# Inverse's input in two buffers, loaded 14 steps ahead; S before the filter in the ring; the last accumulator added by TensorE

## The chip, the cores and the metric

The kernel runs on one core of one Trainium2 chip. The metric is the device time of one execution in microseconds (us). Each execution computes the whole chain below once, from inputs in HBM to the output in HBM.

## The reference, cut to what matters

```python
X = np.fft.rfft(x, axis=1)                      # x: 8 x 3072 x 256, float32
y = np.fft.irfft(X * (filt_r + 1j * filt_i), n=3072, axis=1)
t = y.reshape(8 * 3072, 256)
h = np.maximum(t @ w_in, 0.0)                   # w_in 256 x 2048
z = h * h @ w_out                               # w_out 2048 x 256
logits = z @ phi                                # phi 256 x 32
d = softmax(logits, axis=0)                     # over all 24576 tokens
slot_in = (d.T @ z).reshape(8, 4, 256)          # 8 experts, 4 slots each
slot_out[e] = np.maximum(slot_in[e] @ w1[e], 0) @ w2[e]
out = softmax(logits, axis=1) @ slot_out
```

The softmax over tokens runs over the whole sequence of all batches, so the kernel carries a running maximum, a running sum and a running weighted accumulator, and rescales them as it goes.

## The kernel before, in words

The tokens go through in 48 chunks of 512, six to a batch of 3072 tokens. The main loop is over pairs: `pair(P)` does two of the sixteen 128-wide blocks of the hidden layer for a chunk, so a chunk has 8 pairs. Time inside the program is counted in steps, two to a pair, 16 to a chunk. TensorE always has the hidden layer to do (`layer`, lines 594 to 596, three passes each). Everything else is put between these matmuls by a written timetable: five lists of (step, function, arguments), called streams, are sorted by step, and `run_streams` emits what has come due. So the order of instructions on each engine is fixed when the program is built; at run time each engine works through its own list in that order, and waits where an instruction's input or buffer is not ready.

Around the hidden layer stand, by batch:

- the forward transform: `load_x` (line 143) brings x in, `mm_a` (165) transforms, `store_a` (181) writes the result S to HBM. S is read again in another layout by `load_s2` (206), the filter by `load_f2` (198), their small matrices by `load_w` (190). `mm_b` (299) does the second half, `filt` (310) multiplies by the filter, `join` (319) adds;
- the inverse: `load_v` (194) brings a matrix, `mm_g2` (218) does the first half, `store_g2` (240) writes the result G to HBM. Then, for each chunk, `load_g` (460) reads 512 KB of G into the tile `gin`; `mm_y` (514) does the last half, and `even_y`, `unfold`, `lead_y`, `rest_y` (522, 531, 539, 546) make of it the hidden layer's input `xo`. `mm_y` of a chunk stands 12 steps ahead of the chunk's first hidden block, `rest_y` ends 8.5 steps after `mm_y`;
- the dispatch (`dispatch_events`): the logits of a chunk (663), the softmax numbers, and `slot_in` (793), 32 matmuls that add the chunk's tokens into the 32 slots. They read the hidden values `hT` from a copy in another layout, `hd`, made by 16 DMAs of 256 KB a chunk (`move`, 651). `hd` has one buffer, so the first move of a chunk waits for `slot_in` of the chunk before. `accum` (853) adds the chunk into the accumulator `ac` on VectorE.

All these DMAs but a few are issued by SyncE (SP), one after the other in the order of the timetable. A DMA that has to wait for a buffer or for another DMA's landing holds all that stand behind it on SP.

Buffers that matter: `gin` has one in before (4 KB a partition). The tiles of x, filter, S and of the inverse's result share one tag, `f8`, with three buffers, so each takes the buffer of the third before it; the text calls this the ring. The table `LEAD` holds, for batch 1, batch 2 and all later ones, how many steps ahead of its use each of four loads is asked for: the small matrix, the inverse's matrix, the filter, S.

At the end (from line 1252) the last chunk's `slot_blocks` (810) leave four partial sums in PSUM. They are copied out (1295, 1297), `sum_block` (835) adds them into one PSUM bank `pst`, and VectorE forms `fin`, the accumulator times its scale plus `pst`. `turn_l` (759) turns the logits of the last chunk, `sT` is `fin` turned, and the matmuls of line 1318 read `sT`. The expert layers (1338, 1360) and the output (1405) follow. Weights of the experts are loaded into tiles that have come free.

Of the kernel before, what the change touches and what calls it, by code (L numbers as in the profile page):

```python
# [6 lines left out]
F32 = mybir.dt.float32  # L7
F32R = mybir.dt.float32r
U32 = mybir.dt.uint32
ACTF = mybir.ActivationFunctionType  # L10
ALU = mybir.AluOpType
# [4 lines left out]
D = 256  # L16
# [9 lines left out]
NS = 32  # L26
# [12 lines left out]
def body(tc, x, cA, cAf, fwp, fwd, ivp, inv, flt, cst, w_in, w_out, phi, w1, w2, out):  # L39
    nc = tc.nc  # L40
    sync = nc.sync
    act, vec, gps, pe = nc.scalar, nc.vector, nc.gpsimd, nc.tensor
# [7 lines left out]
    G = {}  # L50
# [6 lines left out]
    first_c, first = pool("first")  # L57
# [34 lines left out]
    ident = cst_t[:, C_ID:C_ID + 128]  # L92
# [361 lines left out]
    def out_events(b, st, late):  # L454

        def load_g(g):
            if b + g:
                t = G["mlp"].tile([128, 4, D], F32, tag="gin", name="gin")
                src, o = (st["G1"], 0) if (b, g) == (0, 1) else (st["G"], 4 * g - 8 * (b == 0))
                sync.dma_start(out=t, in_=src[:, o:o + 4, :])  # L460
            else:
                t = scratch("gi", 1, [128, 4, D])
                sync.dma_start(out=t[0:96], in_=st["Gu"])
                sync.dma_start(out=t[96:128], in_=st["Gz"])
            st["gi", g] = t
# [82 lines left out]
        for g in range(NCB):  # L548
            if 6 * b + g not in (0, 1, 6):
                T = 96 * b + 16 * g - 12  # L550
                late(T - 6.5, load_g, g)
                late(T, mm_y, g)
                late(T + 0.5, even_y, g)
                late(T + 1, unfold, g, ALU.add)
                late(T + 1.5, unfold, g, ALU.subtract)
                for k in range(2):
                    late(T + 5.5 + 2 * k, lead_y, g, k)
                    late(T + 6.5 + 2 * k, rest_y, g, k)
                continue
            T = 96 * b + 16 * g - 4  # L560
            put = late
            if T < 0:
                def put(t, fn, *a):
                    put0(ST["G0"] + ST["Gd"] * (t + 7), fn, *a)
            put(T - (5 if (b, g) == (0, 1) else 3), load_g, g)
            if T < 0:
                put(T - 1, warm)
            for k in range(2):
                put(T + k, mm_ai, g, k)
                put(T + k + 0.5, lead_ai, g, k)  # L570
                put(T + k + 0.5, rest_ai, g, k)
# [123 lines left out]
    run = {}  # L695

    def dispatch_events(c, put):
        q = 16 * (c + 1) + (2 if c else 6)
        st = {}
        dsp = G["dsp"]  # L700
# [127 lines left out]
                act.activation(out=t, in_=p, func=ACTF.Copy)  # L828
            done(p)

        def sum_block(r, p):
            t = st.pop(("sp", r))
            for n in range(4):
                rows = slice(32 * n, 32 * n + 32)
                pe.matmul(
                    p[rows, :].rearrange("p (f r j) -> p f r j", r=4, j=32)[:, :, r, :], s32,
                    t[:, 128 * n:128 * n + 128].rearrange("p (f j) -> p f j", j=32),
                    start=True, stop=True, skip_group_check=True, tile_position=(0, 32 * n),
                )

        def sum_blocks():
            st["S"] = p = side()
            for r in range(4):
                sum_block(r, p)

        def accum():
            p = st["S"]
            if "ac" not in run:
                run["ac"] = dsp.tile([128, 4 * 512], F32, tag="ac", name="ac")
            ac = run["ac"][:, 0:512]  # L850
            if "m" in run:
                z = dsp.tile([128, 1], F32, tag="z", name="z", bufs=2)
                vec.scalar_tensor_tensor(out=ac, in0=ac, scalar=st["sc"], in1=p, op0=ALU.mult, op1=ALU.add)  # L853
                vec.scalar_tensor_tensor(
                    out=z, in0=run["z"], scalar=st["sc"], in1=st["zb"], op0=ALU.mult, op1=ALU.add
                )
            else:
                vec.tensor_copy(ac, p)
                z = st["zb"]
            done(p)  # L860
            run["z"], run["m"] = z, st["nm"]
# [31 lines left out]
        if c == 0:  # L893
            put(q + 7.5, slot_blocks)
            for r in range(4):
                put(q + 9 + .5 * r, keep_block, r)
            put(q + 11.5, sum_blocks)
            put(q + 12, accum)
        else:
            put(q + 7.5, slot_in)  # L900
            put(q + 9, accum)
# [199 lines left out]
    with tc.manual_schedule():  # L1101
        put, late = stream("fft"), stream("late")
        st = {}
# [23 lines left out]
        for n in range(4):  # L1127
# [2 lines left out]
                wput(WO[n][1][k], conv_wo, n, k)  # L1130

        LEAD = [
            [[5.5] * 4, [3.5] * 4, [5.5] * 4, [5] * 4],
            [[5.5, 7.5, 15.25, 15.25], [6.5, 12.5, 13.5, 13.5], [5.5, 5.5, 10, 10], [5, 5, 9.5, 9.5]],
            [[20.25] + [15.25] * 3, [13.5] * 4, [20.5, 10, 10, 10], [8, 9.5, 9.5, 9.5]],
        ]

        opened = False
# [6 lines left out]
        for b in range(1, NB):  # L1145
            st = {}
# [8 lines left out]
        for c in range(NCH - 1):  # L1155
            dispatch_events(c, stream("dsp"))
            if c:
                for n in range(4):
                    t = 0.5 * (n // 2)
# [7 lines left out]
        dsp, mlp = G["dsp"], G["mlp"]  # L1167
# [4 lines left out]
        def bank(tag):  # L1172
            return G["ps"].tile([128, 512], F32, tag=tag, name="pt")
# [41 lines left out]
        for P in range(NP + 2):  # L1215
            if P == 11:
                open_fft()
            if P == 48 * (NB - 1):
                G["fft_c"].__exit__(None, None, None)
                G["w1_c"], w1p = pool("w1p")  # L1220
                for n in range(6):
                    m = 4 if n < 5 else 2
                    w1t.append(w1p.tile([128, m * 512], F32, tag=f"w{n}", name="w1t"))
                    load_experts(w1t[-1], m, 0)
            if P == NP - 7:
                early = G["mlp"].tile([128, 8 * D], F32, tag="xo", name="wx", bufs=2)
                load_experts(early, 0, 3)
                c_two = early[:, 3 * D:4 * D].rearrange("p (t s) -> p t s", s=NS)
                sync.dma_start(out=c_two, in_=c_dr[:, 0:8, :])
                sk = early[:, 4 * D:].bitcast(F32R).rearrange("p (g t a s) -> p g t a s", g=2, t=4, a=4)  # L1230
            if P > NP - 8:
                j, odd = divmod(P - NP + 7, 2)
                if odd:
                    for nm in "HL":
                        n1 = int(j == 0)
                        load_experts(wp.tile([128, 1024], F32, tag=f"i{nm}{j}", name="wx"), n1, 4 - 2 * n1)
            if P == NP - 4:
                big = G["dsp"].tile([128, FT * CH], F32, tag="hT", name="wx", bufs=1)
                load_experts(big[:, 0:4096], 8, 0)
                wor = big[:, 4096:].rearrange("p (f d) -> p f d", d=D)  # L1240
                for n in range(4):
                    sync.dma_start(
                        out=wor[32 * n:32 * n + 32],
                        in_=wo_dr[512 * n:512 * n + 512, :].rearrange("(k j) d -> j k d", j=32),
                    )
            if P == NP - 2:
                ct_two = mlp.tile([128, 2, 4, 128], F32R, tag="gin", name="ct")
                go(stack, stack)
            pair(P)

# [7 lines left out]
        for k in range(2):  # L1258
# [8 lines left out]
        slot_blocks()  # L1267
        go(keep, keep)
        hs = [[mlp.tile([128, 512], F32, tag=f"h{k}", name="hs", bufs=5) for k in range(2)]]
        vec.tensor_tensor(out=st["zb"], in0=st["zs"][:, 0:1], in1=st["zs"][:, 1:2], op=ALU.add)  # L1270
        fz = dsp.tile([128, 1], F32, name="fz")
        vec.scalar_tensor_tensor(
            out=fz, in0=run["z"], scalar=st["sc"], in1=st["zb"], op0=ALU.mult, op1=ALU.add
# [14 lines left out]
        for n in range(3):  # L1288
            load_call(n)
        pst = bank("L")  # L1290
        parts = hs[0] + [dsp.tile([128, 512], F32, tag=t, name="sp") for t in ("lp", "et")]
        for r in range(4):
            p = st["S"][r]
            if r % 2:
                vec.tensor_copy(parts[r], p)
            else:
                act.activation(out=parts[r], in_=p, func=ACTF.Copy)
            done(p)
            st["sp", r] = parts[r]
            sum_block(r, pst)  # L1300
        fin = dsp.tile([128, 512], F32, tag="eT", name="fin", bufs=2)
        vec.scalar_tensor_tensor(
            out=fin, in0=run["ac"][:, 0:512], scalar=st["sc"], in1=pst, op0=ALU.mult, op1=ALU.add
        )
        turn_l()
        sT = dsp.tile([128, 16, NS], F32, tag="lp", name="sT")
        vec.transpose(sT.rearrange("p f s -> p (f s)"), fin)
        load_experts(dsp.tile([128, 512], F32, tag="et", name="wx"), 0, 2)
        load_experts(dsp.tile([128, 4 * 512], F32, tag="ac", name="wx"), 0, 7)
        row_max()  # L1310
        row_exp()
        row_out()
# [2 lines left out]
        p = bank("s0")  # L1315
# [253 lines left out]
```

## Time and profile before

| | before |
|---|---|
| median of 3 runs | 1973.51 us (1968.02 to 1975.3) |
| the profiled execution's own time | 1969.8 us |
| its span, first to last instruction | 1968.0 us |
| mean granted TensorE clock (share of full speed) | 0.974 |
| TensorE busy (matmul) | 1855.7 us, 94% |
| VectorE, ScalarE, GpSimd busy | 61%, 52%, 39% |
| DMA busy share in the body | about 0.75 |

PE is TensorE's matmuls, PEld its weight loads, DVE VectorE, ACT ScalarE, POOL GpSimd, SP SyncE, SPq its DMA issues. A wait in square brackets is the idle time of the engine just ahead of an instruction, with the one that ended it. The granted clock has two levels here: 1.00 is 2.4 GHz and 0.50 is 1.2 GHz.

### The profile page before, as it was taken

To read this page: it belongs to the slowest core of one execution; us is meant where nothing else is said; L and a number is where in the kernel's file an instruction comes from. 1 tells how busy PE (TensorE), PEld (TensorE's weight loads), DVE (VectorE), ACT (ScalarE), POOL (GpSimd) and SP (SyncE) were. 2 spreads that over 40 slices of the span, in tenths; PEclk is the share of its full clock that TensorE was granted. 3 is DMA by queue.
4 is the path that set the end of the run, shared out by engine and by line. 5 is a ranking of instruction groups with operands and counts; after the bars stand their busy time and mean duration, and the time that the engine had idled before them with its cause. 6 is when DMAs were issued, how large, how long until landed. Compare 5 with 4: busy or idle time off the path is not lost.

```text
span 1968.0 us, 42096 instructions
## 1 busy us (share of the span) xinstructions
PE 1855.7 (94%) x16324; PEld 1220.7 (62%) x16324; DVE 1207.0 (61%) x2267; ACT 1033.2 (52%) x1930; POOL 773.7 (39%) x812
## 2 busy tenths in 40 slices
PE   8999999989999999989999999998998999899987
PEld 6656566656666666666665666666565666466555
DVE  7856556556656566556665566555665566455558
ACT  6755445545545465545554465454554455455535
POOL 4044444334435344434434444344443343233224
PEclk9999999999999999999999999999999999999989
DMA  8678779867866796777876696677867756664989
GB/s 298 215 196 234 224 203 263 230 180 214 257 180 176 193 276 178 218 219 211 254 205 166 173 275 198 176 218 205 261 180 202 205 136 196 194 171 125 232 322 379
DMA packets 245799, 425.04 MB, mean 216 GB/s; under 512 B 25696, under 2 KB 103648, under 8 KB 245600
## 3 DMA queue, kind: packets, MB, share of 16 engines
q1 hardware_dynamic: 244728, 421.13, 74.1%
q8 instruction: 130, 2.13, 0.4%
q10 hardware_dynamic: 728, 1.15, 0.2%
q14 instruction: 69, 0.57, 0.1%
q0 software_dynamic: 144, 0.07, 0.0%
HBM read 151.71 MB, written 77.59 MB: 117 GB/s over the span
## 4 chain that ended last, share of the span: by engine, by line
PE 68%; DMA 13%; SPq 8%; DVE 5%; issue 3%; ACT 2%; POOL 1%; DVEq 0%; POOLq 0%; ACTq 0%
PE p L594 15%; PE p L596 13%; PE p L595 13%; PE sd L793 8%; DMA gin<-G 8%; PE L L663 7%; SPq L651 4%; PE sd L514 3%; PE sd L299 3%; SPq L206 2%; PE sd L165 2%; DVE hT L622 2%; DMA f<-x 1%; ACT h L601 1%; PE sd L218 1%
## 5 line engine op out<-in xcount | busy, mean ns | idle before, releaser
L601 ACT ACTIVATE h<-p 128x512 f32<-128x512 f32 x768 | 458.7, 597 | 572.0 <-PE p L596 555.2
L605 POOL TENSOR_TENSOR h<-h 128x512 f32<-128x512 f32 x375 | 393.0, 1048 | 914.5 <-ACT h L601 820.1
L622 DVE STREAM_TRANSPOSE hT<-h 128x512 f32<-128x512 f32 x736 | 489.9, 693 | 370.9 <-ACT h L603 313.4
L594 PE MATMUL p<-xo,wiH 128*128 128x512 f32 x1534 | 636.0, 415 | 0.0
L596 PE MATMUL p<-xo,wiL 128*128 128x512 f32 x1534 | 613.1, 400 | 0.0
L595 PE MATMUL p<-xo,wiH 128*128 128x512 f32 x1534 | 613.0, 400 | 0.0
L594 PEld LDWEIGHTS p<-xo,wiH 128*128 128x128 f32 x1534 | 294.1, 192 | 158.9 <-issue 82.1
L596 PEld LDWEIGHTS p<-xo,wiL 128*128 128x128 f32 x1534 | 293.5, 191 | 69.9
L595 PEld LDWEIGHTS p<-xo,wiH 128*128 128x128 f32 x1534 | 294.6, 192 | 60.1
L603 ACT ACTIVATE h<-h 128x512 f32<-128x512 f32 x393 | 248.4, 632 | 12.5
L319 POOL TENSOR_TENSOR u<-u 128x256 f32<-128x256 f32 x224 | 160.7, 740 | 126.0 <-DVE u L310 126.0
L663 PE MATMUL L<-h,wf 128*32 128x512 f32 x1536 | 186.4, 599 | 2.2 <-DVE wf L1017 1.8
L793 PE MATMUL sd<-hd,eT 128*32 128x512 f32 x1472 | 169.1, 597 | 8.6 <-DMA hd<-hT 8.6
L310 DVE TENSOR_TENSOR u<-sd,f 128x512 f32<-128x512 f32 x240 | 152.8, 675 | 10.9 <-PE sd L299 9.2
L793 PEld LDWEIGHTS sd<-hd,eT 128*32 128x32 f32 x1472 | 48.3, 111 | 120.9 <-issue 106.3
L546 POOL TENSOR_TENSOR xo<-gin,xo 128x512 fp32r<-128x512 f32 x90 | 119.0, 1322 | 0.0
L514 PE MATMUL sd<-cst_t,gin 64*64 64x64 f32 x2880 | 60.5, 242 | 56.5 <-DMA gin<-G 56.5
L531 DVE TENSOR_TENSOR gin<-gin,sd 128x512 f32<-128x512 f32 x90 | 60.0, 667 | 86.7 <-ACT gin L522 79.9
L228 ACT ACTIVATE f<-sd 128x512 f32<-128x512 f32 x112 | 61.1, 610 | 86.4 <-PE sd L218 86.4
L514 PEld LDWEIGHTS sd<-cst_t,gin 64*64 64x64 f32 x2880 | 54.3, 154 | 73.9 <-issue 73.6
L853 DVE SCALAR_TENSOR_TENSOR ac<-ac,sc,sd 128x512 f32<-128x512 f32 x46 | 34.4, 748 | 107.1 <-PE sd L793 107.1
L663 PEld LDWEIGHTS L<-h,wf 128*32 128x32 f32 x1536 | 40.4, 109 | 95.1 <-issue 89.7
(159 smaller groups left out, 1600.2 us busy)
## 6 DMA issues: line engine op xcount, KB each, us to landing
hd<-hT SPq DMA_DIRECT2D x736, 256.0 KB
f<-flt SPq DMA_DIRECT2D x28, 1024.0 KB
gin<-G SPq DMA_DIRECT2D x47, 512.0 KB
out<-w1t SPq DMA_DIRECT2D x47, 512.0 KB
f<-x SPq DMA_DIRECT2D x84, 256.0 KB
S<-f SPq DMA_DIRECT2D x42, 512.0 KB
f<-S SPq DMA_DIRECT2D x112, 192.0 KB
G<-f SPq DMA_DIRECT2D x112, 192.0 KB
```

What stands on the lines that cost most here:

```text
L310: vec.tensor_tensor(out=u, in0=p.rearrange("p (h d) -> p h d", d=D), in1=f[:, 2 * r + k:2 * r + k + 1, :].to_broadcast([128, 2, D]), op=AL ...
L319: gps.tensor_tensor(out=a[:, h, :], in0=a[:, h, :], in1=b[:, 1 - h, :], op=ALU.add if h else ALU.subtract)
L514: pe.matmul(y.rearrange("p (q a t) -> p a q t", q=2, a=4)[:, a], t[rows, a, o:o + 64], cI[rows, 0:64], start=True, stop=True, skip_group_c ...
L594: pe.matmul(p, wh, x[:, 0, kk, :], start=(kk == 0), stop=False)
L595: pe.matmul(p, wh, x[:, 1, kk, :], start=False, stop=False)
L596: pe.matmul(p, wl, x[:, 0, kk, :], start=False, stop=(kk == 1))
L601: act.activation(out=h, in_=p, func=ACTF.Relu, scale=2.0 ** -8)
L603: act.activation(out=h, in_=h, func=ACTF.Square)
L605: gps.tensor_tensor(out=h, in0=h, in1=h, op=ALU.mult)
L622: vec.transpose(hT[c, f // 8][:, f // 4 % 2, :, o:o + 128], h2[P, k].rearrange("p (b t) -> p b t", b=4))
L663: pe.matmul(lg[c][32 * n:32 * n + 32, :], wf[:, f, :], h2.pop((P + n // 2, n % 2)), start=(f < 4), stop=(f >= FT - 4), tile_position=(0, 3 ...
L793: pe.matmul(S[32 * n:32 * n + 32, :], e[:, 32 * t:32 * t + 32], v, start=(t == 0), stop=(t == 3), tile_position=(0, 32 * n),)
```

## The change: what it does

1. `gin` gets two buffers, and `load_g` is asked for 14 steps ahead of `mm_y` in place of 6.5 (never before step 13.5). The chunks 0, 1 and 6, which go another way, keep their times.
2. `LEAD`: S is asked for ahead of the filter. In batch 1 by half a step, in batch 2 from its second stage on, and from batch 3 on in every stage but the first S comes 15.25 steps ahead (9.5 before) and the filter stays at 10. In batch 1 the filter goes from 5.5 to 5 steps ahead, S from 5 to 5.5.
3. The accumulator's tile shrinks from 8 to 4 KB a partition, which pays for `gin`'s second buffer. Expert weights that were loaded into its tail at the end go into the free `gin` buffer two pairs before the loop ends.
4. At the end the accumulator is scaled in place on VectorE, and TensorE puts it into `pst` with a matmul by the identity before the sums are added on top. `fin` is gone, `sT` is turned straight from `pst`, and `turn_l` stands behind it.
5. `accum` of the first chunk is called at the end of `sum_blocks`, half a step earlier.

```diff
         def load_g(g):
             if b + g:
-                t = G["mlp"].tile([128, 4, D], F32, tag="gin", name="gin")
+                t = G["mlp"].tile([128, 4, D], F32, tag="gin", name="gin", bufs=2)
...
-                late(T - 6.5, load_g, g)
+                late(max(T - 14, 13.5), load_g, g)
                 late(T, mm_y, g)
...
-        def sum_block(r, p):
+        def sum_block(r, p, first=True):
...
-                    start=True, stop=True, skip_group_check=True, tile_position=(0, 32 * n),
+                    start=first, stop=True, skip_group_check=True, tile_position=(0, 32 * n),
...
             for r in range(4):
                 sum_block(r, p)
+            accum()
...
-                run["ac"] = dsp.tile([128, 4 * 512], F32, tag="ac", name="ac")
+                run["ac"] = dsp.tile([128, 2 * 512], F32, tag="ac", name="ac")
...
-            put(q + 12, accum)
...
-            [[20.25] + [15.25] * 3, [13.5] * 4, [20.5, 10, 10, 10], [8, 9.5, 9.5, 9.5]],
+            [[20.25] + [15.25] * 3, [13.5] * 4, [20.5, 10, 10, 10], [8, 15.25, 15.25, 15.25]],
...
-                ct_two = mlp.tile([128, 2, 4, 128], F32R, tag="gin", name="ct")
+                ct_two = mlp.tile([128, 2, 4, 128], F32R, tag="gin", name="ct", bufs=2)
+                load_experts(mlp.tile([128, 4 * D], F32, tag="gin", name="wx", bufs=2), 0, 4)
...
+        ac = run["ac"][:, 0:512]
+        vec.tensor_scalar(out=ac, in0=ac, scalar1=st["sc"], scalar2=None, op0=ALU.mult)
...
         pst = bank("L")
+        pe.matmul(pst, ident, ac, start=True, stop=False, skip_group_check=True)
...
-            sum_block(r, pst)
-        fin = dsp.tile([128, 512], F32, tag="eT", name="fin", bufs=2)
-        vec.scalar_tensor_tensor(
-            out=fin, in0=run["ac"][:, 0:512], scalar=st["sc"], in1=pst, op0=ALU.mult, op1=ALU.add
-        )
+            sum_block(r, pst, False)
+        sT = dsp.tile([128, 16, NS], F32, tag="lp", name="sT")
+        vec.transpose(sT.rearrange("p f s -> p (f s)"), pst)
         turn_l()
-        sT = dsp.tile([128, 16, NS], F32, tag="lp", name="sT")
-        vec.transpose(sT.rearrange("p f s -> p (f s)"), fin)
...
-        load_experts(dsp.tile([128, 4 * 512], F32, tag="ac", name="wx"), 0, 7)
+        load_experts(dsp.tile([128, 2 * 512], F32, tag="ac", name="wx"), 0, 3)
```

Three places show how the instructions stand. The first is SP's list over one chunk of batch 3 with a filter in it, which repeats in three chunks of each batch; `hd<-hT` are the moves for `slot_in`, `gin<-G` the inverse's load, `f<-S` and `f<-flt` the loads of S and filter. Before:

```order
L651 DMA hd<-hT 128x1x512 x8
L198 DMA f_6351<-flt 128x2x1024
L206 DMA f_6358<-S 48x4x256 x4
L460 DMA gin<-G 128x1024
L651 DMA hd<-hT 128x1x512 x8
L879 DMA c_dr<-co 128x128
L194 DMA iv<-inv 128x256 x2
L240 DMA G<-f_6490 48x4x256 x4
L190 DMA fw<-fwd 48x256 x4
```

The same stretch of SP's list now:

```order
L651 DMA hd<-hT 128x1x512 x8
L198 DMA f_6358<-flt 128x2x1024
L651 DMA hd<-hT 128x1x512 x8
L880 DMA c_dr<-co 128x128
L194 DMA iv<-inv 128x256 x2
L240 DMA G<-f_6490 48x4x256 x4
L460 DMA gin<-G 128x1024
L190 DMA fw<-fwd 48x256 x4
L206 DMA f_6667<-S 48x4x256 x4
```

The loads of `gin` and of S have left the place between the two groups of moves and stand after the second, behind the store of G and ahead of the next chunk's moves.

The second place is SP's list at the end of a batch's forward work, where the store `G<-f` is the batch's last and the load `gin<-G` behind it now is the same batch's first. Now:

```order
L240 DMA G<-f_5330 48x4x256 x4
L460 DMA gin<-G 128x1024
L181 DMA S<-f_5207 128x1024 x2
L143 DMA f_5505<-x 64x2x512 x4
L143 DMA f_5518<-x 64x2x512 x4
L651 DMA hd<-hT 128x1x512 x8
```

Before, that load stood behind the eight moves; it reads what the store ahead of it writes, so SP now waits there for the store's landing.

The third place is VectorE's list at the end, after the copies of the last partial sums. Before, and then now:

```order
L1295 COPY sp<-sd 128x512
L1302 SCALAR_TENSOR_TENSOR fin<-ac,sc,pt 128x512
L759 STREAM_TRANSPOSE lt<-sd 32x128 x4
L1307 STREAM_TRANSPOSE sT<-fin 128x512
L779 TENSOR_REDUCE rm<-lt 128x4
```

```order
L1299 COPY sp<-sd 128x512
L1306 STREAM_TRANSPOSE sT<-pt 128x512
L759 STREAM_TRANSPOSE lt<-sd 32x128 x4
L779 TENSOR_REDUCE rm<-lt 128x4
L780 TENSOR_TENSOR cl<-lt,rm 128x128
```

`fin` has gone, and `sT` stands ahead of the four turns of the logits instead of behind them.

## Rows read from the trace of the kernel before

**Rows 1.** The page's head: span, then busy time and share of each engine.

```profile
span 1968.0 us, 42096 instructions
PE 1855.7 (94%) x16324; PEld 1220.7 (62%) x16324; DVE 1207.0 (61%) x2267; ACT 1033.2 (52%) x1930; POOL 773.7 (39%) x812
```

**Rows 2.** Waits of PE, whole span: us in total, times, longest us.

```profile
PE sd L514 <- DMA gin<-G: 56.5, 17, 5.7
PE sd L793 <- DMA hd<-hT: 8.6, 1, 8.6
...
PE sd L299 <- DMA f<-S: 3.2, 3, 2.5
```

**Rows 3.** Windows over the twelve half-clock stretches: the second, and the sum of all.

```profile
core 0: us, PE busy (x) PEld busy (x) DVE busy (x) ACT busy (x) POOL busy (x), PEclk, DMA share, GB/s
...
430.49:437.32 6.83, 5.24 (x72) 4.48 (x73) 1.03 (x2) 1.83 (x3) 0.00 (x0) 0.50 0.83 234
...
sum 64.86, PE 57.02 PEld 48.11 DVE 15.97 ACT 18.92 POOL 0.00; mean PE 4.75 PEld 4.01 DVE 1.33 ACT 1.58 POOL 0.00
```

**Rows 4.** Chain of waits in order of time, four slot_in: start us, us, what.

```profile
403.68 3.43 PE sd L793 x32
...
447.37 3.43 PE sd L793 x32
...
483.24 3.43 PE sd L793 x32
...
518.78 3.43 PE sd L793 x32
```

**Rows 5.** Timeline of SP, two stretches: start us, us, engine, line, what.

```profile
213.01 0.42 SPq L198 DMA_DIRECT2D f<-flt  x1
213.47 2.16 SPq L206 DMA_DIRECT2D f<-S  x4
...
407.18 8.22 SPq L651 DMA_DIRECT2D hd<-hT  x8
415.44 0.81 SPq L198 DMA_DIRECT2D f<-flt  x1
416.30 4.49 SPq L206 DMA_DIRECT2D f<-S  x4
420.89 0.41 SPq L460 DMA_DIRECT2D gin<-G  x1
421.40 11.45 SPq L651 DMA_DIRECT2D hd<-hT  x8
...
435.98 2.55 SPq L240 DMA_DIRECT2D G<-f  x4
```

**Rows 6.** Waits of SP's DMA queue, whole span: us in total, times, longest us.

```profile
SPq L651 <- PE sd L793: 324.3, 44, 12.2
SPq L651 <- DMA f<-flt: 56.8, 24, 4.7
...
SPq L206 <- DMA S<-f: 20.2, 10, 4.0
```

**Rows 7.** Timeline of PE in batch 1, with the wait ahead of it.

```profile
219.45 0.59 PE L299 MATMUL sd<-f,fw 48*32 48x256 f32 x2 [2.46 <-DMA f<-S]
```

**Rows 8.** Timeline of all engines at the end of the loop.

```profile
1861.41 1.13 PE L719 MATMUL sd<-lp,cst_t 128*128 128x512 f32 x2 [0.69 <-ACT lp L708]
...
1870.93 0.75 DVE L1302 SCALAR_TENSOR_TENSOR fin<-ac,sc,pt 128x512 f32<-128x512 f32 x1 [0.55 <-PE pt L835]
1871.59 1.28 DVE L759 STREAM_TRANSPOSE lt<-sd 32x128 f32<-32x128 f32 x4
...
1873.72 3.10 PE L1318 MATMUL pt<-wx,sT 128*32 128x256 f32 x32 [2.86 <-DVE sT L1307]
```

**Rows 9.** Windows over two other half-clock stretches, columns as in rows 3.

```profile
222.20:229.10 6.90, 6.37 (x41) 4.27 (x42) 2.63 (x6) 1.23 (x2) 2.83 (x4) 0.51 1.05 379
...
1874.33:1884.57 10.24, 9.34 (x59) 3.40 (x52) 3.40 (x7) 0.72 (x2) 0.00 (x0) 0.50 0.99 319
```

More of the change, by code (lines that the diff above doesn't have):

```diff
@@ L1132, in body @@
         LEAD = [
-            [[5.5] * 4, [3.5] * 4, [5.5] * 4, [5] * 4],
-            [[5.5, 7.5, 15.25, 15.25], [6.5, 12.5, 13.5, 13.5], [5.5, 5.5, 10, 10], [5, 5, 9.5, 9.5]],
-            [[20.25] + [15.25] * 3, [13.5] * 4, [20.5, 10, 10, 10], [8, 9.5, 9.5, 9.5]],
+            [[5.5] * 4, [3.5] * 4, [5] * 4, [5.5] * 4],
+            [[5.5, 7.5, 15.25, 15.25], [6.5, 12.5, 13.5, 13.5], [5, 5.5, 10, 10], [5.5, 13, 15.25, 15.25]],
+            [[20.25] + [15.25] * 3, [13.5] * 4, [20.5, 10, 10, 10], [8, 15.25, 15.25, 15.25]],
         ]
```

## The prediction

> **What bounds the kernel now.** I read the page first: TensorE (PE) is busy 1855.7 of 1968.0 us, and no other engine passes 62% [rows 1]. So PE sets the time, and the question is what its idle 112 us wait for. The list of PE's waits answers that: 56.5 us, half of it, is line 514 waiting for the load of `gin`, 17 times, at most 5.7 us; the next largest is one wait of 8.6 us for `hd` [rows 2]. The reader should see that this is one cause in one place of the timetable.
>
> The granted clock comes next. Behind twelve of the 17 waits it stands at 0.50 (1.2 GHz) for a stretch; the windows over these twelve stretches add up to 64.9 us, in which PE is busy 57.0 [rows 3]. Work done at 0.50 takes twice as long as at 1.00 (2.4 GHz), so half of the busy time, 28.5 us, is lost there, behind the waits and on top of them.
>
> The chain of waits checks this. From one slot_in to the next a chunk takes 43.7 us (403.68 to 447.37), the one after it 35.9, and the third 35.5 (483.24 to 518.78) [rows 4]. The first holds a wait for `gin`, the third holds none and does as much PE work (the hidden layer and two of the transform's pieces). The excess of 8.2 us is the 5.7 us wait plus 5.24 / 2 = 2.6 us of slow clock behind it [rows 2, 3].
>
> Why `gin` is late is in SP's timeline of that chunk: the first eight moves for slot_in are issued from 407.18, behind them the filter (1 MB), S and, at 420.89, `gin`; then eight more moves [rows 5]. Its 512 KB queue behind all these bytes and are wanted about 5 us before they are there.
>
> **The change, part by part.**
>
> *gin in two buffers, 14 steps ahead.* The load now stands behind the store of G (435.98 to 438.53 in that chunk [rows 5]) for the chunk after. A chunk without waits takes 35.5 us for 16 steps, 2.2 us a step; 14 steps are 31 us, against the some 14 us that 6.5 steps give now. The second buffer is free by then: the tile two before is done 8.5 steps after its own use, 9.5 steps ahead of this load. All 17 waits should go: 56.5 us. With them goes what follows them, 28.5 us. What is late next? After `gin` PE has no wait that comes again in every chunk [rows 2], so nothing waits close behind it; I book no new wait in the body, and put what could be there into the rivals.
>
> The Trainium skill speaks on the second term ("TensorE: Matmul & The Clock Gate", section on HAM oscillation): PE waiting on DMA is throttled to half its clock, and the penalty is half of the throttled time. By that rule the twelve stretches would give back 64.9 / 2 = 32.4 us, an estimate with that page, and the sum would be 3.9 us lower. The rows show less, since 64.9 - 57.0 = 7.8 us of the stretches lie in the waits themselves, which are counted already.
>
> *SP's new waits.* Nothing is added in DMAs; the 47 loads are the same. But the moved ones stand ahead of the moves now: S with 4.49 us and `gin` with 0.41 us of SP's time [rows 5] pass in front of the next chunk's first move. That move waits for slot_in anyway, 324.3 us in 44 waits, 7.4 us a chunk [rows 6]: this slack covers the 4.9 us. If it were gone, the moves would come up to 4.9 us later; but the second eight come as much earlier, since S and `gin` no longer stand in front of them. In 7 chunks (the first load of a batch) SP also waits for the landing of the store of G just ahead. The nearest row is S read back behind its own store: 20.2 us in 10 waits, 2.0 us each, 4.0 at most [rows 6]. Bounds 0 and 7 x 4.0 = 28 us of PE time; I take 0, since behind that place SP waits for slot_in too, and x, the load it holds, is folded steps later.
>
> Here a rule of the skill speaks against the change ("DMA: Bandwidth & Descriptors", on where the fixed cost of about 2 us goes): completion, above all of a write to HBM, makes up most of a DMA's fixed time, so waiting for a store is dear. By that page's figures the four stores of 768 KB would hold SP 2.0 us plus 1.8 us of moving, an estimate of 3.8 us. The row's longest, 4.0 us, agrees, and the sum stays, since 7.4 us of slack is more than either.
>
> *S ahead of the filter.* In batch 1 one second half of the transform waits 2.46 us for S [rows 7], whose load is issued 0.46 us behind the filter's 1 MB (213.01 and 213.47) [rows 5]; a half-clock stretch with 6.37 us of busy PE follows [rows 9]. Asked for first, S lands earlier by what the filter moves. Gain between 0 (the filter then holds VectorE's multiplication) and 2.5 + 6.4 / 2 = 5.6 us; I take 4, nearer to the upper end, since PE does not read the filter. From batch 3 on S moves out of the crowded stretch between the moves; PE waits for S only 3.2 us in the whole span [rows 2], so it saves nothing itself. In the ring S now takes the buffer of the S before it, as the loads ahead of it on SP wait for the same matmuls: no new wait.
>
> *First accum half a step earlier.* VectorE's order is the same; 0.
>
> *The end.* PE waits 2.86 us between the last sums and line 1318 [rows 8]. On the chain there, `fin` (0.75) and the turns of the logits (1.28) go away from in front of `sT`: 2.0 us. The new matmul by the identity has a like in line 719, the same shape and type: 1.13 us in two passes [rows 8]. It stands where PE waits for the copies of the partial sums, so it adds between 0 and 1.1 us; I take 0.5, the middle. Net 1.5 us, bounds 0.9 and 2.0. VectorE's scaling of `ac` runs while PE does the partial sums: 0. Behind this wait follows 10.24 us at half clock with 9.34 us of busy PE [rows 9], worth 4.7 us if the shorter wait no longer brings it on and 0 if it does; I take half, 2.3. The end gives 3.8 us, bounds 0.9 and 6.7.
>
> **The sum.** 56.5 + 28.5 + 4 + 3.8 = 92.8 us. The profiled execution took 1969.8 us (span 1968.0), so it would take 1877.0. The median of the runs shown is 3.7 us above the profiled execution, and I add this: 1880 us, 4.7% faster. Its own range: the two small terms at their upper ends (5.6 and 6.7) give 1876, and a few us more where other waits shrink along with these, 1870; the two at their lower ends give 1887, and one or two waits for `gin` that stay, 1892.
>
> **The rivals.**
>
> *The moves become the limit.* With shorter chunks slot_in may wait for `hd`. In the chunk of rows 5 SP finishes the second eight moves at 432.85 and slot_in starts at 447.37 [rows 4], 14.5 us later. The chunk loses 8.2 us, the moves gain 4.9 us on SP, so 11.2 us stay for landing: enough. Against that, SP is held by DMAs in flight: moves wait for the filter's landing 56.8 us in 24 waits [rows 6], and the filter now stands directly ahead of them. If the 4.9 us is not won, 14.5 - 8.2 = 6.3 us stay for landing and queueing, which is thin. Say the 18 chunks with a filter of batches 2 to 7 each wait 2.5 us: 45 us back, 1880 + 45 = 1925 us. Chance 0.15.
>
> *The load still comes late.* If SP reached the new place late, because the store of G ahead of it waits or because the loads share one queue, the waits would stay in part. Against it: 31 us of lead, and SP has 7.4 us to spare in each chunk. If half the waits and half of the slow clock stayed, 1880 + 42 = 1922; if nearly all, about 1965 (1880 + 85). Chance 0.06, most of it at the lower figure.
>
> *Slower.* One mechanism: SP's list is in order, and `gin` behind the store of G and S behind the matmuls that free its ring buffer hold the first moves of the next chunk until slot_in starves. The price is the wait seen once, 8.6 us [rows 2]: in the 18 chunks with a filter 155 us, so 1880 + 155 = 2035 us. It decides from 92.8 / 18 = 5.2 us a chunk on, and first the 7.4 us of slack must be used up. The delays listed, 4.9 us and in 7 chunks 2 to 4 us more, come close to the slack in those 7 only. Chance 0.04.
>
> *More than the sum.* The one wait of 8.6 us for `hd` [rows 2] goes too because the DMA traffic is spread, and the small terms are at their upper ends: 1876 - 8.6 and some slow clock behind it, about 1865. Chance 0.05.
>
> **How the numbers follow.** Forecast 0.70, moves 0.15, late load 0.06, slower 0.04, more 0.05. Predicted is the forecast's 1880. The range 1862 to 1918 holds the forecast, the better case and a part of the moves' case (those with up to 2.1 us a chunk); outside are the rest of that case, the late load and the slower one, some 0.18. A difference under 0.5% (10 us) cannot be told from none, the runs before spread 7 us. Faster: 0.70 + 0.15 + 0.05 and most of the late load, 0.94; same 0.02; slower 0.04.
>
> **What would show it.** In the profile after: no row, or a row of a few us, for line 514 waiting for `gin`; granted clock near 0.99 on average, and no half-clock stretch in the body but around batch 1 and the one `hd` wait; all chunks with a filter at 35 to 36 us from slot_in to slot_in; SP's wait of the moves for slot_in still there, about 2 us shorter; S in batch 1 no longer waited for; `sT` directly behind the sums, with line 1318 about 1.5 us nearer to them. The forecast is wrong if line 793 shows waits for `hd` in many chunks (moves), if line 514 keeps more than 15 us (late load), or if SP's first move of a chunk waits for nothing of slot_in any more.

## The result, and the profile after

The changed kernel took 1884.03 us (median of 4 runs, 1880.15 to 1886.42) against 1972.63 us of the kernel before (1968.02 to 1975.3): a ratio of 0.9551, 95% interval 0.9526 to 0.9576. The forecast was 1880, its range 1862 to 1918. The profiled executions differ by as much: spans of 1968.0 and 1878.2 us, 89.8 us apart.

The head of the page after (span, then busy time and share of each engine) answers to [rows 1]:

```profile
span 1878.2 us, 42103 instructions
PE 1824.0 (97%) x16326; PEld 1196.4 (64%) x16326; DVE 1206.0 (64%) x2267; ACT 1034.8 (55%) x1930; POOL 774.4 (41%) x812
```

PE did the same work (two matmuls more) in 31.7 us less of busy time, and idles 54.2 us where it idled 112.3. So 58.1 us of the gain is waiting that is gone, and 31.7 is work done at a higher clock. Apart from PE's own weight loads (PEld, 24.3 us less), no engine's busy time moved by more than 1.6 us.

What PE waits for after (us in total, times, longest us), against [rows 2]:

```profile
PE sd L793 <- DMA hd<-hT: 6.9, 1, 6.9
...
PE sd L723 <- DVE lo L712: 6.0, 7, 2.3
PE sd L218 <- DMA iv<-inv: 4.1, 2, 3.1
```

Line 514 and the load of `gin` are in the list no more: all 17 waits went. The longest one left is the single wait for `hd`. The half-clock stretches within the span add up to 23.6 us in five places, against 100.5 in eighteen. Line 723 waits 2.6 us more for VectorE than before (3.4).

The chain of waits in order of time (start, us, what) shows the chunk length, as in [rows 4]:

```profile
359.41 3.43 PE sd L793 x32
...
395.04 3.43 PE sd L793 x32
...
430.65 3.43 PE sd L793 x32
...
466.94 3.43 PE sd L793 x32
```

A chunk with a filter takes 35.6 us where 43.7 was seen before; it has become as long as the chunk without a wait (35.5). The one at 430.65, which loads x instead of a filter, takes 36.3.

SP's timeline of the first of these chunks, after, answers to [rows 5]:

```profile
362.91 8.32 SPq L651 DMA_DIRECT2D hd<-hT  x8
371.27 0.60 SPq L198 DMA_DIRECT2D f<-flt  x1
371.97 9.15 SPq L651 DMA_DIRECT2D hd<-hT  x8
...
384.01 2.46 SPq L240 DMA_DIRECT2D G<-f  x4
386.56 0.79 SPq L460 DMA_DIRECT2D gin<-G  x1
387.45 2.13 SPq L190 DMA_DIRECT2D fw<-fwd  x4
389.71 3.17 SPq L206 DMA_DIRECT2D f<-S  x4
398.53 2.58 SPq L651 DMA_DIRECT2D hd<-hT  x3
```

Between the two times eight moves only the filter is left; `gin` and S stand behind the store of G, and behind them SP has 5.7 us (392.9 to 398.5) in which it issues nothing. What SP's queue waits for, after, against [rows 6]:

```profile
SPq L651 <- PE sd L793: 252.2, 39, 11.1
...
SPq L206 <- DMA S<-f: 32.7, 12, 6.3
...
SPq L460 <- DMA G<-f: 15.6, 12, 2.8
SPq L651 <- DMA f<-flt: 15.0, 17, 2.0
```

The moves still wait for slot_in, 6.5 us each time (7.4 before). The wait for the store of G in front of `gin` is new. The moves' waits behind the filter fell from 56.8 to 15.0.

### The profile page after: what moved, and what is told of

Its sections match the earlier page's. It is cut to its first block, busy times and chain, and to the rows that moved or that the text cites. A ratio compares the mean times of both kernels' runs of the same rounds, so it can differ in the third digit from the quotient of the medians.

```text
span 1878.2 us, 42103 instructions
## 1 busy us (share of the span) xinstructions
PE 1824.0 (97%) x16326; PEld 1196.4 (64%) x16326; DVE 1206.0 (64%) x2267; ACT 1034.8 (55%) x1930; POOL 774.4 (41%) x812
## 4 chain that ended last, share of the span: by engine, by line
PE 84%; DMA 6%; DVE 3%; SPq 3%; issue 2%; ACT 1%; POOL 0%; DVEq 0%; ACTq 0%
PE p L594 18%; PE p L596 17%; PE p L595 17%; PE sd L793 9%; PE L L663 8%; PE sd L299 3%; PE sd L514 2%; PE sd L218 2%; PE sd L165 2%; SPq L651 2%; DMA f<-x 2%; DMA hd<-hT 1%; DMA f<-flt 1%; DVE ct L1204 1%; PE pt L1193 1%
## 5 line engine op out<-in xcount | busy, mean ns | idle before, releaser
L594 PE MATMUL p<-xo,wiH 128*128 128x512 f32 x1534 | 626.6, 408 | 0.0
L596 PE MATMUL p<-xo,wiL 128*128 128x512 f32 x1534 | 605.8, 395 | 0.0
L595 PE MATMUL p<-xo,wiH 128*128 128x512 f32 x1534 | 605.1, 394 | 0.0
L594 PEld LDWEIGHTS p<-xo,wiH 128*128 128x128 f32 x1534 | 288.5, 188 | 156.5 <-issue 81.8
L596 PEld LDWEIGHTS p<-xo,wiL 128*128 128x128 f32 x1534 | 288.7, 188 | 68.5
L595 PEld LDWEIGHTS p<-xo,wiH 128*128 128x128 f32 x1534 | 289.2, 188 | 58.7
L712 DVE TENSOR_TENSOR lo<-L,lp 128x512 fp32r<-128x512 f32 x47 | 32.2, 685 | 73.3 <-ACT lp L711 73.2
L156 POOL TENSOR_TENSOR f<-f 128x512 f32<-128x512 f32 x42 | 54.1, 1288 | 57.0 <-DVE u L155 38.0
L769 DVE STREAM_TRANSPOSE eT<-et 32x128 f32<-32x128 f32 x184 | 72.3, 393 | 1.9
```

The source lines that it names most:

```text
L594: pe.matmul(p, wh, x[:, 0, kk, :], start=(kk == 0), stop=False)
L595: pe.matmul(p, wh, x[:, 1, kk, :], start=False, stop=False)
L596: pe.matmul(p, wl, x[:, 0, kk, :], start=False, stop=(kk == 1))
```

## The experiments

Each ratio is to the kernel before, timed on the same chip. The kernel before ran between 1959.8 and 1988.4 us over these comparisons, so the ratios tell more than the times.

### Which edit does it

**`gin` alone**: the changed kernel, with the old table of leads (the new end stays in).

```diff
-            [[5.5] * 4, [3.5] * 4, [5] * 4, [5.5] * 4],
-            [[5.5, 7.5, 15.25, 15.25], [6.5, 12.5, 13.5, 13.5], [5, 5.5, 10, 10], [5.5, 13, 15.25, 15.25]],
-            [[20.25] + [15.25] * 3, [13.5] * 4, [20.5, 10, 10, 10], [8, 15.25, 15.25, 15.25]],
+            [[5.5] * 4, [3.5] * 4, [5.5] * 4, [5] * 4],
+            [[5.5, 7.5, 15.25, 15.25], [6.5, 12.5, 13.5, 13.5], [5.5, 5.5, 10, 10], [5, 5, 9.5, 9.5]],
+            [[20.25] + [15.25] * 3, [13.5] * 4, [20.5, 10, 10, 10], [8, 9.5, 9.5, 9.5]],
```

Expected: 

> The changed kernel with the old LEAD table: gin in two buffers and 14 steps ahead, but S still asked for behind the filter, between the two groups of moves. My theory (what counts is gin's own place on SP, ahead of filter, S and moves): no wait of line 514, batch 1's wait for S back (2.5 us and its slow clock), 1884 + 4 = 1888 us, 1882 to 1896. Rival S (S's 4.5 us of SP time and 768 KB between the move groups are what makes things late): slot_in now waits for hd in the chunks with a filter, 2 us each, 1884 + 36 = 1920 us.

Measured: 1889.97 us, ratio 0.9568 (0.9513 to 0.9623). No wait in line 514. In batch 1 the wait for S is back:

```profile
PE sd L299 <- DMA f<-S: 3.9, 2, 3.1
```

So the early load of `gin` is enough for the 17 waits, as the forecast had it, and the time is where it was expected.

**S alone**: the kernel before, with the new table of leads and nothing else (the diff above read the other way, in the old kernel).

Expected: 

> The kernel before with the new LEAD table alone: gin keeps one buffer and 6.5 steps, S goes ahead of the filter and out of the stretch in front of gin. My prediction as written (S's move saves nothing by itself from batch 3 on): about 1965 us, line 514 still waiting some 50 us. Rival S: S is what stands in front of gin, 4.5 us on SP and 768 KB; the 17 waits (mean 3.3 us, longest 5.7) shrink by about that, to at most 10 us in sum, and the slow clock goes with them: about 1895 us, 1885 to 1915.

Measured: 1889.17 us, ratio 0.957 (0.9518 to 0.9622). Here the rival was right and the forecast's own reading wrong: with one buffer and 6.5 steps, `gin` is in time once S isn't in front of it. SP's timeline of this kernel, then PE's row for line 514 of the same chunk:

```profile
398.87 1.78 SPq L206 DMA_DIRECT2D f<-S  x4
405.93 8.12 SPq L651 DMA_DIRECT2D hd<-hT  x8
414.10 0.88 SPq L198 DMA_DIRECT2D f<-flt  x1
415.09 1.07 SPq L460 DMA_DIRECT2D gin<-G  x1
416.26 8.28 SPq L651 DMA_DIRECT2D hd<-hT  x8
...
425.10 1.16 PE L514 MATMUL sd<-cst_t,gin 64*64 64x64 f32 x64
```

The load is issued 10.0 us ahead of its use and there is no wait in brackets behind the row. Either edit alone takes away the same waits; they share one gain and don't add. By the ratios both together are 3 to 4 us better than either, and since the intervals overlap that is not certain.

**The second buffer alone**: the changed kernel, with `gin` asked for 6.5 steps ahead and the old table, so the second buffer and the new end stay in.

```diff
-                late(max(T - 14, 13.5), load_g, g)
+                late(T - 6.5, load_g, g)
...
```

Expected: 

> The changed kernel with gin asked for 6.5 steps ahead again and the old LEAD table: the second buffer, the smaller accumulator and the new end alone. My theory: SP's list in the body is the one of before, so the waits of line 514 stay at 50 to 60 us; the end gives 4 to 9 us: 1973 - 6 = 1967 us, 1962 to 1973. Rival (the second buffer itself frees the load): under 1900 us.

Measured: 1972.08 us, ratio 0.9984 (0.9949 to 1.0019): no change that can be told from none, as expected. PE's waits:

```profile
PE sd L514 <- DMA gin<-G: 61.9, 17, 5.0
```

The buffer wasn't what the load waited for; it only makes room to ask earlier. This run also holds the new end, and so bounds what that can be worth: by the interval, 0.5% or some 10 us at most.

**The old end** in the changed kernel: `fin`, the scaling behind the sums, and the turns of the logits ahead of `sT`, as before.

```diff
-        pe.matmul(pst, ident, ac, start=True, stop=False, skip_group_check=True)
...
-            sum_block(r, pst, False)
+            sum_block(r, pst)
+        fin = dsp.tile([128, 512], F32, tag="eT", name="fin", bufs=2)
...
```

Expected: 

> The changed kernel with the old end (fin on VectorE, turn_l ahead of sT, no matmul by the identity, no scaling of the accumulator in place). My theory: the end costs 1.5 us more for its shorter path and up to 4.7 us for the slow clock behind it: 1884 + 4 = 1888 us, 1885 to 1891. Rival (the end is hidden or made up by the clock): 1884, within 1 us.

Measured: 1882.44 us, ratio 0.9532 (0.9479 to 0.9585), no different from the changed kernel: the rival was right. Where the saving goes is in PE's timelines. The changed kernel:

```profile
1776.68 4.46 PE L810 MATMUL sd<-hT,eT 32*32 32x512 f32 x128 [1.18 <-DVE eT L773]
...
1784.12 2.60 PE L1318 MATMUL pt<-wx,sT 128*32 128x256 f32 x32 [0.91 <-DVE sT L1306]
1787.86 0.63 PE L1326 MATMUL pt<-cst_t,af 128*128 128x32 f32 x4 [1.14 <-DVE af L1323]
```

With the old end (one line further down in the code):

```profile
1782.28 4.46 PE L810 MATMUL sd<-hT,eT 32*32 32x512 f32 x128 [1.18 <-DVE eT L773]
...
1791.41 2.86 PE L1319 MATMUL pt<-wx,sT 128*32 128x256 f32 x32 [2.87 <-DVE sT L1308]
1794.85 1.06 PE L1327 MATMUL pt<-cst_t,af 128*128 128x32 f32 x4 [0.59 <-DVE af L1324]
```

From the start of line 810 to the multiplication with `sT` it is 7.4 us against 9.1: 1.7 won. One step on, to the multiplication with `af`, 11.2 against 12.6: 1.4 left, since `af` now stands on VectorE behind the turns and the row softmax that used to be done sooner. To the first matmul of line 1405 (1406 with the old end; it starts at 1810.62 and 1816.40) it is 33.9 against 34.1, so 0.2 us is left there. Most of the loss stands at line 1360 (1361 with the old end), the second expert layer: its last matmuls take from 1801.71 to 1808.40, 6.7 us, against 5.3 in the run with the old end, and among them the changed kernel waits for a load of expert weights:

```profile
PE pt L1360 <- DMA wx<-w: 0.7, 1, 0.7
```

The run with the old end doesn't have this wait, but it is 3.5 us in the kernel with `gin` alone (new end) and 2.3 in the one with S alone (old end): it differs from run to run with either end, and a saving ahead of it can be lost there. In the kernel before the same way takes 35.8, with a half-clock stretch of 10.2 us on it against 6.8 here with the same old end: that part of the gain at the end came without the end's edit.

### Why `gin` was late, and what a wait costs

**The filter behind `gin`**: the kernel before, with the filter's lead cut from 10 to 8 (from batch 2 on). Moving S takes away 768 KB and 4.5 us of SP's time; moving the filter takes away 1 MB and 0.8 us.

```diff
-            ... [5.5, 5.5, 10, 10], [5, 5, 9.5, 9.5]],
-            ... [20.5, 10, 10, 10], [8, 9.5, 9.5, 9.5]],
+            ... [5.5, 5.5, 8, 8], [5, 5, 9.5, 9.5]],
+            ... [20.5, 8, 8, 8], [8, 9.5, 9.5, 9.5]],
```

Expected: 

> The kernel before with one edit: from batch 3 on the filter is asked for 8 steps ahead instead of 10, which puts its 1 MB (0.81 us of SP's time to issue) behind gin in the crowded stretch; S (768 KB, 4.49 us of SP's time) stays ahead of gin, and gin has one buffer and 6.5 steps. Moving S away alone gave 1889. Theory of bytes: gin is late because of the data queued ahead of it; 1 MB less ahead is worth more than 768 KB less, so the waits of line 514 nearly go (under 10 us) and the time is 1885 to 1900. Theory of the issuer: gin is late because SP is held by S's four descriptors for 4.5 us; then the filter's 0.81 us matter little, the waits stay at 4 us each (40 to 60 us) and the time is 1940 to 1970. Of slots between: 1 MB of the filter then competes with the second eight moves, and hd may come late; a wait of line 793 in several chunks would show it.

Measured: 1894.02 us, ratio 0.9583 (0.954 to 0.9626), no wait in line 514: the theory of bytes gave this, and the theory of the issuer is out as the only cause. SP's timeline and PE's row of line 514, this kernel:

```profile
415.29 3.38 SPq L206 DMA_DIRECT2D f<-S  x4
418.78 0.38 SPq L460 DMA_DIRECT2D gin<-G  x1
...
420.50 1.74 SPq L198 DMA_DIRECT2D f<-flt  x1
...
426.32 1.16 PE L514 MATMUL sd<-cst_t,gin 64*64 64x64 f32 x64
```

And PE's row in the kernel before, whose `gin` was issued at 420.89 [rows 5]:

```profile
432.08 1.99 PE L514 MATMUL sd<-cst_t,gin 64*64 64x64 f32 x64 [5.67 <-DMA gin<-G]
```

Before, 11.2 us passed from the issue of `gin` to its use, which was at once when it came. With the filter behind it, it is there within 7.5 us, and the issue is 2.1 us earlier. Of the wait of 5.67 us the earlier issue explains 2.1, the shorter way of the load at least 3.6.

That the bytes count for more holds for this edit only. Each load reports the landing of its parts by semaphore, and from these updates the way of every load can be read. Over the 17 loads that were waited for in the kernel before, and the same 17 in the other two kernels, the means are:

| | issue to PE's coming to line 514 | issue to landing | wait |
|---|---|---|---|
| before | 6.05 us | 9.24 us | 3.32 us |
| S moved | 9.83 us | 8.57 us | 0 |
| filter moved | 7.64 us | 6.29 us | 0 |

Moving S lets SP issue the load 3.8 us further ahead of its use, and shortens the load's way by 0.7. Moving the filter shortens the way by 2.95 and brings the issue 1.6 further ahead. The wait was 3.3 us, so either is enough, for two different reasons.

**A larger dose**: the changed kernel with `gin` asked for 3 steps ahead.

```diff
-                late(max(T - 14, 13.5), load_g, g)
+                late(T - 3, load_g, g)
```

Expected: 

> The changed kernel with gin asked for 3 steps ahead instead of 14, so that it stands behind half of the second eight moves too; all else as changed. It puts the late load back in a larger dose, to test how a wait is paid for. My accounting: time after = 1884 + waits of line 514 + half of the busy time in the half-clock stretches behind them. With 3 steps the load has 6.7 us of lead (14 us in the kernel before) and 1 MB of moves more ahead of it, so I expect waits of 4 to 8 us in most of the 45 chunks, 200 to 300 us in all, and half-clock stretches behind most of them, another 60 to 130 us: 2150 to 2310 us; the test is that the measured time agrees with 1884 plus what this profile shows by the accounting, to within 20 us. Rival: the slow clock costs nothing of its own, since a stretch at half clock lies in the wait; then the time is 1884 plus the waits alone. Second rival: the load is late only when the filter or S stand ahead of it; these are elsewhere or no more than 1 MB here, so the waits stay under 50 us and the time under 1950.

Measured: 1999.05 us, ratio 1.0125 (1.0075 to 1.0175): 1.25% slower than the kernel before, and far below the 2150 to 2310 expected. The dose itself came out under half of what I expected: PE's waits of this kernel:

```profile
PE sd L514 <- DMA gin<-G: 95.1, 38, 17.0
```

The windows over its 21 half-clock stretches, summed (us, then busy time of each engine; here and in the next row the last window runs 2.2 us past the end of the span):

```profile
sum 100.03, PE 73.02 PEld 56.82 DVE 27.02 ACT 26.42 POOL 5.50; mean PE 3.48 PEld 2.71 DVE 1.29 ACT 1.26 POOL 0.26
```

The same sum for the changed kernel:

```profile
sum 25.78, PE 13.53 PEld 6.64 DVE 5.00 ACT 1.58 POOL 1.32; mean PE 2.71 PEld 1.33 DVE 1.00 ACT 0.32 POOL 0.26
```

The test was the accounting, and it holds. The waits for `gin` are 95.1 us more, the wait for `hd` (6.9) is gone, and half of the extra busy time at half clock is (73.0 - 13.5) / 2 = 29.7: 117.9 us, where the spans differ by 114.1 and the medians by 115.0. The waits alone would make 88.2 and 1972 us, which the interval (1990 to 2010 us, from the ratio) leaves out. PE's busy time itself shows the cost of the slow clock: it is 27.4 us longer (1851.4 against 1824.0), where half of the busy time at half clock gives 29.7. The second rival fell too: the waits were not under 50 us.

### What is left, and a better version

**The expert weights in portions**: the changed kernel, with the 22 loads of 256 KB in six portions, one every two pairs. (The expectation says steps; `P` counts pairs, so it is four steps.)

```diff
-                for n in range(6):
-                    m = 4 if n < 5 else 2
-                    w1t.append(w1p.tile([128, m * 512], F32, tag=f"w{n}", name="w1t"))
-                    load_experts(w1t[-1], m, 0)
+            if P >= 48 * (NB - 1) and P % 2 == 0 and len(w1t) < 6:
+                n = len(w1t)
+                m = 4 if n < 5 else 2
+                w1t.append(w1p.tile([128, m * 512], F32, tag=f"w{n}", name="w1t"))
+                load_experts(w1t[-1], m, 0)
```

Expected: 

> The changed kernel with the first expert weights (22 tiles of 256 KB, all asked for at one place ahead of the last batch) asked for in six portions, one every two steps. PE's one wait for hd, 6.9 us, and a half-clock stretch of 6.83 us stand behind that place. Mine: this is the burst's doing; both go, 7 + 3 = 10 us, 1874 (1870 to 1878). Rival: hd is late there for another reason (the store of G, the order of the moves), or the wait moves to another chunk: 1884, with a wait of 5 to 9 us still in line 793.

Measured: 1872.48 us, ratio 0.9482 (0.9449 to 0.9514), below the interval of the changed kernel. The changed kernel around its one wait for `hd`, SP first and then PE:

```profile
1562.90 12.59 SPq L651 DMA_DIRECT2D hd<-hT  x12
1575.53 15.46 SPq L1085 DMA_DIRECT2D w1t<-w  x22
1591.39 3.23 SPq L651 DMA_DIRECT2D hd<-hT  x4
...
1598.71 5.24 PE L793 MATMUL sd<-hd,eT 128*32 128x512 f32 x26 [6.88 <-DMA hd<-hT]
```

With the weights in portions:

```profile
1564.28 12.25 SPq L651 DMA_DIRECT2D hd<-hT  x12
1576.57 2.94 SPq L1085 DMA_DIRECT2D w1t<-w  x4
1579.62 3.85 SPq L651 DMA_DIRECT2D hd<-hT  x4
...
1592.21 3.62 PE L793 MATMUL sd<-hd,eT 128*32 128x512 f32 x32
```

22 issues held SP for 15.5 us in front of the last four moves. PE came to line 793 at 1591.83 (1598.71 less the wait), 0.4 us after SP had begun to issue these moves, and that was the wait: in portions it is gone, and so is the half-clock stretch behind it. The time is in the expected range.

**x ahead of the moves**: the changed kernel, with the first load of x of a batch 4.5 steps earlier.

```diff
-                when = ([(-35, -31, -26), (-23, -19, -14.5), (-22.5, -15.5, -10)], [1.5, 22, 38, 54], [17.5, 33.5, 49.5, 65.5])
+                when = ([(-39.5, -31, -26), (-23, -19, -14.5), (-22.5, -15.5, -10)], [1.5, 22, 38, 54], [17.5, 33.5, 49.5, 65.5])
```

Expected: 

> The changed kernel with the first load of x of each batch from 3 on asked for 39.5 steps ahead instead of 35, which puts it in front of the first eight moves of its chunk. Chunks with x take 36.3 to 38.3 us against 35.6, and VectorE waits 27.5 us for x and PE, behind it, 6.0 us for VectorE at line 723. Mine: the waits at line 723 fall under 1.5 us and these chunks come to 35.6: 1878 (1874 to 1881). Rival: x in front holds up the moves, hd comes late in these chunks: line 793 waits in up to 5 chunks, 1890 to 1905. Second rival: the chunks with x are longer by their work, not by the wait: 1884.

Measured: 1878.45 us, ratio 0.951 (0.9476 to 0.9544). That overlaps with the changed kernel, so the time alone does not show the gain. PE's waits at line 723:

```profile
PE sd L723 <- DVE lo L712: 1.9, 2, 1.0
```

Its chain of waits:

```profile
431.05 3.43 PE sd L793 x32
...
466.68 3.43 PE sd L793 x32
```

The wait of 6.0 us has fallen to 1.9 (under 1.5 was expected), but this wait differs from run to run: with x in its old place it is 4.1 us in the run with the old end and 3.1 in the one with portions. The chunks say more: the first one with x now takes 35.6 us (36.3 before the edit), and so do all five of them, which take 36.2 to 38.2 in the changed kernel and 35.8 to 37.0 in those two runs. That is 6 us, or 3.5 to 5 against the two runs.

**All three**: portions, x, and two loads of `iv` in batch 1 earlier.

```diff
-            [[5.5] * 4, [3.5] * 4, [5] * 4, [5.5] * 4],
+            [[5.5] * 4, [5, 3.5, 3.5, 6], [5] * 4, [5.5] * 4],
...
```

Expected: 

> The changed kernel with three edits at once: the first expert weights asked for in six portions (alone 1872.5), the first load of x of each batch 4.5 steps earlier (alone 1878.5, against 1884.0 for the changed kernel), and in batch 1 two loads of the inverse constant (iv) 1.5 and 2.5 steps earlier, for which PE waits 4.1 us in two waits with a half-clock stretch of 3.4 us behind. Mine: the causes are apart from one another, so their gains add: 11.6 + 5.6 + 4.1 + 1.5 = 22.8 us, 1861 (1858 to 1866), with no wait for hd, iv or at line 723 left over 1.5 us. Rival: they overlap, as the two halves of the change did, and the time stays at 1868 to 1873, with a wait of one of the three kinds still in the profile.

Measured: 1863.54 us (1861.63 to 1865.69), ratio 0.942 (0.9388 to 0.9453), the fastest version and 1.1% below the changed kernel by the medians. The time is in the expected range. No wait for `hd` or `iv` is among PE's longest; line 723 keeps 2.6 us in three waits, the longest 1.6. Here the gains nearly add (20.5 us of 22.8 by the medians), as one would expect of waits that stand at different places of the timetable.

## Why the prediction was right, and where it was not

- *`gin` in two buffers, 14 steps ahead: 56.5 us.* Right: no wait of the 17 is left, and the early load alone does it (1890).
- *Slow clock behind it: 28.5 us.* Right. PE's busy time fell by 31.7, which is this term and what batch 1 and the end brought. The larger dose bears out the sum with half the busy time (117.9 worked out, 114.1 measured). The Trainium skill ("TensorE: Matmul & The Clock Gate", section on HAM oscillation) counts half of the whole throttled time; for the 74.2 us of extra stretches in that run this would be 37.1 us and a sum of 125.3, an estimate by that rule, further from the 114.1 than the sum by busy time.
- *"From batch 3 on S moves out of the crowded stretch ...; PE waits for S only 3.2 us in the whole span, so it saves nothing itself."* This step failed. Moving S alone took the kernel to 1889 and left no wait at line 514, since S delayed `gin`, not PE: without S in front, `gin` was issued 3.8 us further ahead of its use. I had read who waits for S, and not who stands behind it on SP, although the first part had said that `gin` queues behind these bytes. The total came out right because the gain had been booked already, under `gin`: two edits, one wait.
- *S ahead of the filter in batch 1: 4 us (0 to 5.6).* Right in kind, but the cause is only in part the one I gave. The chunk that holds it took from 198.18 to 241.14, 43.0 us, and 46.0 before; 3.1 us. In the three other runs with the same batch 1 it takes 42.7 to 44.1. The table alone doesn't do it, though: there the chunk takes 47.1, with 4.0 us of waiting for `iv` in place of S; nor does `gin` alone, with 45.9. Why it takes both wasn't tested. A new small wait took the place of the old one: the product `u`, since the filter is now the later load. The chain after:

```profile
198.18 3.43 PE sd L793 x32
...
241.14 3.43 PE sd L793 x32
```

The chain before:

```profile
198.13 3.43 PE sd L793 x32
244.16 3.43 PE sd L793 x32
```

The new wait in PE's timeline after, to be held against [rows 7]:

```profile
232.82 2.09 PE L218 MATMUL sd<-u,iv 32*64 32x256 f32 x64 [1.69 <-POOL u L319]
```

- *The end: 3.8 us (0.9 to 6.7).* Mis-sized: line 1318 came 1.7 us nearer, as worked out (1.5), but 0.2 us of it was left at line 1405, and no gain can be measured. I followed the chain to `sT` and stopped there; what VectorE had been made to do later, the turns, stood in front of `af`, and behind that, line 1360 was slower and waited for a load of expert weights. The stretch at half clock did shrink, from 10.2 to 3.4 us, but 3.4 us of that came with the old end too.
- *SP's new waits: 0.* Right, and the rival of the moves fell. The load of S does wait longer in its new place (32.7 us in 12 for the store of S, 20.2 in 10 before), but in SP's idle time: 6.5 us a chunk of it remained, and the moves' waits behind the filter fell where that rival needed them to grow. The store of G held `gin` in 12 loads, not 7, but for 1.3 us each, below the 2.0 I took as the nearest row. By the figures of the Trainium skill ("DMA: Bandwidth & Descriptors", on the fixed cost of about 2 us) it would be some 3.8 us, an estimate; no wait of this kind was longer than 2.8. The Trainium skill gives them there for DMAs that GpSimd issues, and for the whole of a DMA, so they don't price what SP, which issues these, is held for.
- *The wait for `hd`, which a rival let go with the rest.* It stayed, with 6.9 us of its 8.6. Its cause was one issue of 22 loads, as the run with portions showed.

The sum was 92.8 us, and the spans differ by 89.8. From line 810 to 1405 the end is 1.9 us shorter than before (35.8 and 33.9, most of it not by the edit) where 3.8 was booked, and the chunk of batch 1 3.1 where 4 was; line 723 waits 2.6 us more (3.4 before, 6.0 after, and it differs from run to run), and the wait for `hd` is 1.7 us shorter. That makes 3.7 less, a sum of 89.1. So the total came out right partly by luck: the end's share came for the most part without the end's edit.

## What to carry to other kernels

When a load is late, list everything that stands ahead of it in its queue, with bytes and issue time, and move whichever is easiest: any one of them may be enough, and then the others give little more. Bytes in front make the load's own way longer; issues in front make it start later; the wait is what the two leave together. Ask of a transfer not only who waits for it, but also who waits behind it. And follow a shortened chain past the first wait it shortens, to the point where another engine or load decides.

## What was not expected of the hardware

- A 512 KB load took 11.2 us from issue to use with 1 MB of filter and 768 KB of S issued just ahead, and at most 7.5 us with the filter issued behind it instead. Over the 17 loads that were late, the mean way to landing was 9.2 and 6.3 us.
- Waits and half-clock stretches don't go one to one. Of the 38 waits for `gin` of 2.5 us on average in the run with the larger dose, 15 had a stretch at 0.50 behind them; of the 17 waits of 3.3 us in the kernel before, twelve.
- SP can starve PE by the time that it takes to issue: 22 loads took it 15.5 us, 0.7 us each, the moves behind them started too late, and PE stood for 6.9 us.
